# Routing marks and entries built column by column with a scalar per partition, instead of four interleaved columns at a time

## The chip, the cores and the metric

One core of one Trainium2 chip runs the whole program. The metric is device microseconds from launch to end; lower is better. The kernel before takes 689.84 us (median of 3 runs, 689.8 to 689.98).

## What is computed

Attention over 4 batches of 8 heads, 768 positions and 64 features per head, in which each query sees 8 global keys and the last 96 keys, with a linear bias by distance. The result, 3072 tokens of 512 features, goes through a mixture of 8 experts of which each token uses the best two:

```python
logits = x @ w_gate
noisy = logits + log1p(exp(x @ w_noise)) * noise
top2 = np.argpartition(-noisy, 2, axis=1)[:, :2]
top2_w = softmax(noisy at top2)
for e in range(E):
    for k in range(2):
        mask = top2[:, k] == e
        out[mask] += top2_w[mask, k] * (relu(x[mask] @ w1[e]) @ w2[e])
```

## The kernel before, in words

**Attention.** The 24 tiles of 128 tokens are worked through in order, 4 pairs of heads to a tile, two pairs to a turn of the main loop. In a turn TensorE (PE) transposes the attention weights of two pairs (L750), multiplies older ones with the values (L778) and forms the scores of the pairs four further on (L725). VectorE (DVE) adds the bias to the scores and takes the row extreme (L732, once per half pair, followed by a short read of the accumulator); ScalarE (ACT) takes the exponential (L735). After the fourth pair of a tile DVE divides by the row sums (L788 to L790), and PE transposes the tile and forms the gate's logits (L378, L386). Scores and gate products share three PSUM banks in rotation, two for the scores of a turn and one for the gate, so that the scores of pair m are written into the bank out of which DVE read those of pair m - 2. The values' sums have one buffer of their own, which is free again after L790.

**Routing.** The generator `route` turns logits into lists of tokens per expert, in three segments: tiles 0 to 9, 10 to 15 and 16 to 23. Its last part finds for each token and choice a slot, that is an expert's column and a row in it. Per pair of tiles (four choices of 128 tokens each, one product of the matrix multiplier per choice) it builds a `mark` (128 tokens by 128 rows: 1 where the row is the token's) and an `entry` (128 tokens by 64 columns: the token's number where the column is its). Then PE adds up all products mark x entry of the segment (L512), and DVE adds the sum to the table `tab` (L515), from which the lists of tokens are read that the gathers on POOL go by (L521, L527, L288).

A mark is one comparison of 128 x 128 x 4 elements (L502), an entry one comparison of 128 x 64 x 4 (L504) and one multiplication with the tokens' numbers (L506). The fourth dimension, the choice, is innermost, so that a column of one product has a step of 4 elements. `row` and `col` hold the numbers 0 to 127 and 0 to 63, each four times.

**Order of the work.** All engines take their instructions in the program's order. `route` is advanced by its `yield`s: `tick` takes one step between the instructions of the main loop. While the marks are built there is a step after each half pair of scores (four in a turn) and a few more behind them. Within a pair of tiles one step lies behind the mark, one behind the comparison of the entry and one behind its multiplication. So in segments 0 and 1 a step of the marks mostly stands between two L732 on DVE. Segment 2 is taken after the attention, beside the first expert's first layer: `middle` and `after[4]` build the marks of two pairs of tiles at once, and the products L512 are put ahead of the last product of the eighth block of that layer (L1003). Its other DVE work there is L1009 (low half of the hidden layer) and L233 (low half of the second layer's weights). L1058 is the second layer.

Twelve pairs of tiles there are in all: 5, 3 and 4 in the segments, with 20, 12 and 16 products L512. L212 is a later small DVE instruction with a scalar per partition, L177 a 128 x 128 one, L315 and L620 are DVE instructions with constants alone.

Of the kernel before, what the change touches and what calls it, by code (L numbers as in the profile page):

```python
# [10 lines left out]
F32 = mybir.dt.float32  # L11
FR = mybir.dt.float32r
F16 = mybir.dt.float16
# [4 lines left out]
OP = mybir.AluOpType  # L18
AX = mybir.AxisListType

P = 128
NP = 96
TA, TB = 4, 3
TT = TA + TB
# [12 lines left out]
def tile_local_global_attention_then_moe(  # L37
# [13 lines left out]
    nc = tc.nc  # L51
# [6 lines left out]
    E, _, F = w1.shape  # L58
# [3 lines left out]
    NT = B * NB  # L62
# [8 lines left out]
    SW = max(SWS)  # L71

    ctx.enter_context(tc.manual_schedule())
    consts = ctx.enter_context(tc.tile_pool(name="consts", bufs=1))
    small = ctx.enter_context(tc.tile_pool(name="small", bufs=1))
# [4 lines left out]
    gp = wctx.enter_context(tc.tile_pool(name="gp", bufs=1))  # L80
# [28 lines left out]
    turnf = consts.tile([P, E], F32, name="turnf")  # L109
    turni = consts.tile([P, E], I32, name="turni")  # L110
    ids0 = consts.tile([P, 1, TA], I32, name="ids0")
    val16 = consts.tile([P, NT, 2], F16, name="val16")
    row = consts.tile([P, P, 4], F16, name="row")
    col = consts.tile([P, E * (TT + 1), 4], F16, name="col")
    over = consts.tile([P, NT, E], F32, name="over")
    wmx = consts.tile([P, E, 2, 5], F32, name="wmx")
    wex = consts.tile([P, E, 2], F32, name="wex")
# [279 lines left out]
    def route(r):  # L397

        a, z = SEG[r]
        w, sw = z - a, SWS[r % 2]  # L400
        l = lgs[:, a:z]
        u, t, p, ny, po = (small.tile([P, sw, E], F32, name=f"{x}{r % 2}")[:, :w] for x in ("u", "t", "p", "ny", "po"))
        n = l[:, :, E:]
# [30 lines left out]
        for i in range(w + 1):  # L434
# [4 lines left out]
            if i % 2 or r <= CLOSE:  # L439
# [10 lines left out]
                                op=OP.is_equal)  # L450
# [32 lines left out]
        nc.vector.tensor_reduce(sl.rearrange("p t j -> p j t"), oh, op=OP.add, axis=AX.X)  # L483
        yield
        sli = small.tile([P, 2, sw, 2], I32, name=f"sli{r % 2}")[:, :, :w]
        slf = small.tile([P, 2, sw, 2], F16, name=f"slf{r % 2}")[:, :, :w]
        nc.vector.tensor_copy(sli[:, 0], sl)
        nc.vector.tensor_scalar(sli[:, 1], sli[:, 0], 7, None, op0=OP.arith_shift_right)
        yield
# [3 lines left out]
        marks = []  # L493
        K = E * (TT + 1)
        ps = lg[:, HELD * G + (SW + 1) * E:HELD * G + (SW + 1) * E + K]

        for i in range(0, w, 2):
            x = gp.tile([P, P, 4], F16, name="mark", bufs=SW // 2)
            y = gp.tile([P, K, 4], F16, name="entry", bufs=SW // 2)
            here, there = (slf[:, j, i:i + 2].rearrange("p t j -> p (t j)")[:, None] for j in range(2))  # L500
            v = val16[:, a + i:a + i + 2].rearrange("p t j -> p (t j)")[:, None]
            nc.vector.tensor_tensor(x, row, here.to_broadcast([P, P, 4]), op=OP.is_equal)  # L502
            yield "large"
            nc.vector.tensor_tensor(y, col, there.to_broadcast([P, K, 4]), op=OP.is_equal)  # L504
            yield "large"
            nc.vector.tensor_mul(y, y, v.to_broadcast([P, K, 4]))  # L506
            marks += [(x[:, :, k], y[:, :, k]) for k in range(4)]
            yield "marked" if i + 2 in (4, w) else "large"
        for _ in range(4 if r + 1 < len(SEG) else 0):
            yield  # L510
# [5 lines left out]
        if r == CLOSE:  # L516

            nc.vector.tensor_scalar(carry[:, 0:1], carry[:, 0:1], float(CA), None, op0=OP.max)
            x, y = find(None, slice(0, 1), slice(0, TA))
# [9 lines left out]
    def find(to, e, t):  # L529

        v, k = tab[:, e, t], void[:, e, t]
        x, y = (small.tile([P, E, TT + 1], F32, name=f"find{j}")[:, :k.shape[1], :k.shape[2]] for j in range(2))
        nc.vector.tensor_scalar(x, v, 0.0, None, op0=OP.is_equal)
        nc.vector.tensor_scalar(y, v, 0.0, float(DUMP + HALF - 1), op0=OP.is_lt, op1=OP.add)
        nc.vector.tensor_mul(x, x, k)
        nc.vector.tensor_add(y, y, v)
        if to is not None:
            nc.vector.tensor_add(to, x, y)
        return x, y


    with ExitStack() as actx:
# [44 lines left out]
        if windowed:  # L587
# [34 lines left out]
            t = small.tile([P, 1], F32, name="t")  # L622
# [35 lines left out]
        def route_consts():  # L658
            nc.sync.dma_start(noise_s, noise.rearrange("p (t e) -> p t e", e=E))
            nc.vector.memset(upper, 1.0)  # L660
            nc.gpsimd.affine_select(out=upper, in_=upper, pattern=[[1, P]], compare_op=OP.is_gt, fill=0.0,
                                    base=0, channel_multiplier=-1)
            nc.vector.memset(ones, 1.0)
            nc.vector.memset(carry, 0.0)
            nc.gpsimd.memset(zero, 0.0)
            nc.gpsimd.iota(iota_e, pattern=[[0, 1], [1, E]], base=0, channel_multiplier=0,
                           allow_small_or_imprecise_dtypes=True)
            nc.gpsimd.iota(slot0, pattern=[[0, SW], [(TT + 1) * P, E]], base=0, channel_multiplier=0,
                           allow_small_or_imprecise_dtypes=True)
            for h in range(2):  # L670
                nc.gpsimd.iota(val16[:, h * NT // 2:(h + 1) * NT // 2], pattern=[[P, NT // 2], [0, 2]],
                               base=h * (HALF + 1) - HALF, channel_multiplier=1, allow_small_or_imprecise_dtypes=True)
            for t, n, base in (0, TA, 0), (TA, TT + 1 - TA, TA * P - CA):
                nc.gpsimd.iota(void[:, :, t:t + n], pattern=[[0, E], [P, n]], base=base - (DUMP + HALF - 1),
                               channel_multiplier=1, allow_small_or_imprecise_dtypes=True)
            for x in tab, l1, wv, *first:
                nc.vector.memset(x, 0.0)
            for e in range(E):
                nc.gpsimd.memset(room[:, e:e + 1], float(CAPS[e]))

        def mark_consts():
            nc.gpsimd.iota(row, pattern=[[1, P], [0, 4]], base=0, channel_multiplier=0,
                           allow_small_or_imprecise_dtypes=True)
            nc.gpsimd.iota(col, pattern=[[1, E * (TT + 1)], [0, 4]], base=0, channel_multiplier=0,
                           allow_small_or_imprecise_dtypes=True)

        def empty_rows():
# [112 lines left out]
        def whole(g):  # L800
# [60 lines left out]
            for r, (a, z) in enumerate(SEG):  # L861
                if g == z - 1:
                    for _ in route(r):
                        pass

        pending = iter(())
        if not windowed:
            gate_consts()
            route_consts()
            mark_consts()  # L870
            empty_rows()
            for j in range(NZ):
# [15 lines left out]
        else:  # L888
# [3 lines left out]
            for k in range(2, HP):  # L892
                at(k - 2, biases, bias, dist, (2 * k, 2 * k + 1))
            at(4, gate_consts)
            at(10, route_consts)
            at(14, mark_consts)
            at(56, empty_rows)
            for g in range(NT):
                b, i = divmod(g, NB)
                n = g * HP  # L900
                if g + 3 < NT:
                    at(n + 2, load_v, g + 3)
                m = n + HP - 1 + LAG + 1
                if g + 1 < NT:
                    at(m, gate_t, g)
                    at(m + 2, gate_l, g)
                    if g not in held:
                        seen[m + 6] = g
                    elif g + 1 == SEG[CLOSE][1]:
                        then[m + 4] = g  # L910
                    elif m + 4 < NPAIR + LAG:
                        at(m + 4, gate_s, g)
                if i % NBH == 0 and g + NBH < NT:
                    for k in range(NBH):
                        at(n + 4 * k, load_qk, *divmod(g // NBH + 1, 2), k)
                for r, (a, z) in enumerate(SEG):
                    if g == z - 1:
                        routes[m + (4 if g in held else 6)] = [route(r), r, None]
# [427 lines left out]
```

## Time and profile before

| | |
|---|---|
| median of 3 runs | 689.84 us |
| the profiled execution's own time | 687.46 us |
| its span, first to last instruction | 685.7 us |
| granted clock of TensorE, mean | 0.998 |
| attention, routing of segments 0 and 1 | about 0 to 157 us of the span |
| marks of segment 0, 1, 2 on DVE | 108.5 to 116.2, 132.4 to 136.6, 174.2 to 178.9 us |

A matmul's time in the trace includes its way through the array; what one costs in a row of them is the distance of their starts. The same holds on DVE: an instruction starts some 0.08 us before the recorded end of the one ahead of it.

### The profile page before, as it was taken

The page shows a single profiled execution, that of the slowest core. Times are in us where ns is not written, and L with a number is a line of the kernel's source. Part 1 is how long each engine was busy: PE and PEld are TensorE (multiplying, and loading weights), DVE is VectorE, ACT ScalarE, POOL GpSimd, SP SyncE. Part 2 cuts the span into 40 slices and gives each one's busy share as a digit, 9 for nine tenths or more (in the row PEclk, how much of TensorE's full clock was granted, in tenths as well). Part 3 has the DMA queues.
Part 4 walks back from the last instruction along what each step waited for, and adds up shares of the span by engine and source line. Part 5 has one row for each costly group of instructions (what it writes and reads, how often), then busy time and mean ns, then how long its engine had stood idle before and what let it go on. Part 6 is the DMA issues. An engine that isn't in the chain of part 4 may idle for free. (4 is left out here: it accounts for less than half of the span.)

```text
span 685.7 us, 16098 instructions
## 1 busy us (share of the span) xinstructions
PE 674.7 (98%) x6099; PEld 418.9 (61%) x6099; DVE 428.9 (63%) x1455; ACT 366.7 (53%) x830; POOL 195.3 (28%) x208
## 2 busy tenths in 40 slices
PE   7999999999999999999999999999999999999996
PEld 5888878785457665556465746474656466544742
DVE  6686888878958467737572856386547636672600
ACT  6788787885366354625552555256434625442510
POOL 2219510021255712340324032403231331221022
PEclk9999999999999999999999999999999999999999
DMA  8999787949478935954675469438735764471033
GB/s 239 323 309 316 234 253 232 285 151 380 133 137 147 269 124 120 180 139 132 118 171 137 143 99 207 101 124 124 189 93 153 136 168 122 83 107 35 1 40 59
DMA packets 105703, 111.68 MB, mean 163 GB/s; under 512 B 51508, under 2 KB 64468, under 8 KB 105616
## 3 DMA queue, kind: packets, MB, share of 16 engines
q1 hardware_dynamic: 93600, 83.89, 43.1%
q0 software_dynamic: 11472, 26.41, 20.8%
q8 instruction: 50, 0.82, 0.5%
q14 instruction: 37, 0.30, 0.1%
q10 hardware_dynamic: 544, 0.26, 0.1%
HBM read 71.48 MB, written 27.71 MB: 145 GB/s over the span
## 5 line engine op out<-in xcount | busy, mean ns | idle before, releaser
L1003 PEld LDWEIGHTS <-w1h 128*128 128x128 f16 x1024 | 99.7, 98 | 67.2 <-issue 0.8
L1058 PE MATMUL av<-w2h,hh 128*128 128x512 f16 x336 | 127.4, 379 | 0.0
L1058 PE MATMUL av<-w2h,hl 128*128 128x512 f16 x336 | 127.3, 379 | 0.0
L1058 PE MATMUL av<-w2l,hh 128*128 128x512 f16 x336 | 127.3, 379 | 0.0
L1003 PE MATMUL at<-xx,w1h 128*128 128x512 f16 (+5 forms) x512 | 122.9, 330 | 0.6 <-DVE xx L356 0.4
L1003 PE MATMUL sc<-xx,w1h 128*128 128x512 f16 (+5 forms) x512 | 122.8, 330 | 0.0
L1058 PEld LDWEIGHTS <-hh 128*128 128x128 f16 x672 | 65.4, 98 | 76.7
L288 POOL DMA_INDIRECT xg<-xd,ids x54 | 55.2, 1023 | 177.3 <-DVE l L314 92.5
L735 ACT ACTIVATE a<-ns,mx 128x168 f32<-128x168 f32 (+1 forms) x192 | 70.0, 421 | 28.6 <-DVE mx L732 27.4
L1003 PE MATMUL sc<-xx,w1l 128*128 128x512 f16 (+5 forms) x256 | 84.5, 330 | 0.0
L1003 PE MATMUL at<-xx,w1l 128*128 128x512 f16 (+5 forms) x256 | 84.5, 330 | 0.0
L1009 DVE SCALAR_TENSOR_TENSOR hl<-sc,hh 128x512 f16<-128x512 f32 (+5 forms) x64 | 36.2, 565 | 71.7 <-ACT hh L1007 71.7
L171 DVE TENSOR_REDUCE wmx<-raw 128x1 f32<-128x1024 f32 x64 | 75.9, 1206 | 0.0
L1009 DVE SCALAR_TENSOR_TENSOR hl<-at,hh 128x512 f16<-128x512 f32 (+5 forms) x64 | 36.1, 564 | 60.0 <-ACT hh L1007 60.0
L1003 PEld LDWEIGHTS <-w1l 128*128 128x128 f16 x512 | 50.2, 98 | 34.9 <-issue 0.2
L1039 POOL DMA_INDIRECT out_dram<-y,ids x27 | 42.3, 1566 | 102.5 <-ACT y L1038 100.5
L1007 ACT ACTIVATE hh<-at 128x512 f16<-128x512 f32 (+5 forms) x64 | 31.7, 495 | 65.4 <-PE at L1003 65.3
L321 ACT ACTIVATE xp<-xg,up 128x512 f16<-128x512 f32 x48 | 34.2, 720 | 55.5 <-DVE up L315 48.3
L732 DVE CUSTOM_DVE_ANT_0 ns<-sc,bias 128x168 f32<-128x168 f32 (+1 forms) x192 | 53.7, 319 | 16.2 <-PE sc L725 13.0
L1007 ACT ACTIVATE hh<-sc 128x512 f16<-128x512 f32 (+5 forms) x64 | 31.6, 493 | 59.1 <-PE sc L1003 59.1
L1039 POOL DMA_INDIRECT out_dram<-xr,ids x26 | 40.4, 1554 | 74.0 <-ACT xr L1038 73.1
L233 DVE SCALAR_TENSOR_TENSOR w1l<-raw,wsc,w1h 128x512 f16<-128x512 f32 x52 | 36.3, 747 | 36.2 <-ACT w1h L224 35.9
(201 smaller groups left out, 1174.7 us busy)
## 6 DMA issues: line engine op xcount, KB each, us to landing
raw<-in_w SPq DMA_DIRECT2D x28, 1024.0 KB
out_dram<-zero SPq DMA_DIRECT2D x14, 512.0 KB
vs<-in_v SPq DMA_DIRECT2D x24, 260.0 KB
xd<-xr SPq DMA_DIRECT2D x24, 256.0 KB
qs<-in_q SPq DMA_DIRECT2D x23, 256.0 KB
ks<-in_k SPq DMA_DIRECT2D x19, 272.0 KB
raw<-in_w SPq DMA_DIRECT2D x16, 256.0 KB
vp<-in_v SPq DMA_DIRECT2D x20, 195.0 KB
```

What stands on the lines that cost most here:

```text
L171: nc.vector.tensor_reduce(m[:, i:i + 1], t, op=OP.max, axis=AX.X, apply_absolute_value=True)
L233: eng.scalar_tensor_tensor(lo, t, s, hi, op0=OP.mult, op1=OP.subtract)
L288: nc.gpsimd.indirect_dma_start(out=xg[e, t], out_offset=None, in_=xd[:n], in_offset=bass.IndirectOffsetOnAxis(ap=rows(e, t), axis=0), boun ...
L321: nc.scalar.activation(y[:m, :Dm], xg[e, t][:, :Dm], AF.Copy, scale=u)
L732: nc.vector.tensor_tensor_reduce(out=ns[:, s, :w], in0=ps[:, s], in1=bias[:, hp, s] if i else bias0[:, hp, s], scale=-scale, scalar=3e38, ...
L735: nc.scalar.activation(A[m][:, s * w:(s + 1) * w], ns[:, s, :w], AF.Exp, bias=mx[:, s:s + 1], scale=-1.0)
L1003: nc.tensor.matmul(ps, w[e % 2][:, k, fs], xx[c][:, x + k, :z], start=n == 0, stop=n == 3 * KC - 1)
L1007: nc.scalar.activation(hh[c][:, f, :z], ps, AF.Relu)
L1009: nc.vector.scalar_tensor_tensor(hl[c][:, f, :z], ps, 0.0, hh[c][:, f, :z], op0=OP.max, op1=OP.subtract)
L1039: ins = nc.gpsimd.indirect_dma_start(out=out, out_offset=bass.IndirectOffsetOnAxis(ap=rows(e, t), axis=0), in_=y, in_offset=None, bounds_c ...
L1058: nc.tensor.matmul(ps, x[c][:, f, cols], w[e % 2][:, f], start=n == 0, stop=n == 3 * FC - 1)
```

## The change

The four columns of a pair of tiles are made one at a time. A mark's column is a comparison of `row` (128 elements) with a scalar per partition, an entry's column a comparison of `col` (64 elements) with a scalar per partition and, in the same instruction, a multiplication with a second one. Three DVE instructions per pair of tiles become eight. Each product's columns lie side by side in memory. The scalars become 32-bit floats, `row` and `col` a quarter as long. The steps lie behind the third mark, behind the first entry and behind the last entry.

```diff
-    val16 = consts.tile([P, NT, 2], F16, name="val16")
-    row = consts.tile([P, P, 4], F16, name="row")
-    col = consts.tile([P, E * (TT + 1), 4], F16, name="col")
+    val = consts.tile([P, NT, 2], F32, name="val")
+    row = consts.tile([P, P], F16, name="row")
+    col = consts.tile([P, E * (TT + 1)], F16, name="col")
...
-        slf = small.tile([P, 2, sw, 2], F16, name=f"slf{r % 2}")[:, :, :w]
+        slf = small.tile([P, 2, sw, 2], F32, name=f"slf{r % 2}")[:, :, :w]
...
-            x = gp.tile([P, P, 4], F16, name="mark", bufs=SW // 2)
-            y = gp.tile([P, K, 4], F16, name="entry", bufs=SW // 2)
-            here, there = (slf[:, j, i:i + 2].rearrange("p t j -> p (t j)")[:, None] for j in range(2))
-            v = val16[:, a + i:a + i + 2].rearrange("p t j -> p (t j)")[:, None]
-            nc.vector.tensor_tensor(x, row, here.to_broadcast([P, P, 4]), op=OP.is_equal)
-            yield "large"
-            nc.vector.tensor_tensor(y, col, there.to_broadcast([P, K, 4]), op=OP.is_equal)
-            yield "large"
-            nc.vector.tensor_mul(y, y, v.to_broadcast([P, K, 4]))
-            marks += [(x[:, :, k], y[:, :, k]) for k in range(4)]
+            x = gp.tile([P, 4, P], F16, name="mark", bufs=SW // 2)
+            y = gp.tile([P, 4, K], F16, name="entry", bufs=SW // 2)
+            for n in range(8):
+                k = n % 4
+                t, j = i + k // 2, k % 2
+                here, there = (slf[:, m, t, j:j + 1] for m in range(2))
+                if n < 4:
+                    nc.vector.tensor_scalar(x[:, k], row, here, None, op0=OP.is_equal)
+                else:
+                    nc.vector.tensor_scalar(y[:, k], col, there, val[:, a + t, j:j + 1], op0=OP.is_equal, op1=OP.mult)
+                if n in (2, 4):
+                    yield "large"
+            marks += [(x[:, k], y[:, k]) for k in range(4)]
             yield "marked" if i + 2 in (4, w) else "large"
...
-            nc.gpsimd.iota(row, pattern=[[1, P], [0, 4]], base=0, channel_multiplier=0,
+            nc.gpsimd.iota(row, pattern=[[1, P]], base=0, channel_multiplier=0,
-            nc.gpsimd.iota(col, pattern=[[1, E * (TT + 1)], [0, 4]], base=0, channel_multiplier=0,
+            nc.gpsimd.iota(col, pattern=[[1, E * (TT + 1)]], base=0, channel_multiplier=0,
```

## Rows read from the trace of the kernel before

**Rows 1.** The page, part 1: busy time, share of the span, instructions of each engine.

```profile
PE 674.7 (98%) x6099; PEld 418.9 (61%) x6099; DVE 428.9 (63%) x1455; ACT 366.7 (53%) x830; POOL 195.3 (28%) x208
```

**Rows 2.** By stretch: length, busy PE, PEld, DVE, ACT, POOL; marks of segments 0 and 2.

```profile
108.27:126.33 18.06, 18.06 (x338) 14.68 (x338) 16.90 (x109) 14.96 (x42) 0.40 (x2) 1.00 0.87 266
168.40:184.00 15.60, 15.60 (x93) 7.79 (x92) 15.12 (x44) 5.42 (x9) 2.30 (x3) 1.00 0.51 177
```

**Rows 3.** The products L512: engine, op, count, ns min/median/max, first and last start.

```profile
L512 PE MATMUL lg<-entry,mark x48: 223/242/247, 117.4 to 179.9; 128*128 128x64 f16 x48
```

**Rows 4.** Timeline of DVE, segment 0: start us, us, engine, line, op, idle before.

```profile
109.12 0.29 DVE L504 TENSOR_TENSOR entry<-col,slf 128x256 f16<-128x256 f16 x1
109.32 0.33 DVE L732 CUSTOM_DVE_ANT_0 ns<-sc,bias 128x168 f32<-128x168 f32 x1
...
110.03 0.42 DVE L502 TENSOR_TENSOR mark<-row,slf 128x512 f16<-128x512 f16 x1
110.36 0.29 DVE L504 TENSOR_TENSOR entry<-col,slf 128x256 f16<-128x256 f16 x1
110.69 0.29 DVE L506 TENSOR_TENSOR entry<-entry,val 128x256 f16<-128x256 f16 x1
110.91 0.17 DVE L788 TENSOR_SCALAR den<-avb 128x8 f32<-128x8 f32 x1
...
113.32 0.28 DVE L732 CUSTOM_DVE_ANT_0 ns<-sc,bias 128x128 f32<-128x128 f32 x1
...
114.37 0.29 DVE L732 CUSTOM_DVE_ANT_0 ns<-sc,bias 128x128 f32<-128x128 f32 x1 [0.22 <-PE sc L725]
```

**Rows 5.** Timeline of PE: the scores of four turns, merged.

```profile
113.50 0.91 PE L725 MATMUL sc<-ks,qs 64*64 64x128 f32 x15
...
120.29 0.80 PE L725 MATMUL sc<-ks,qs 64*64 64x168 f32 x16
...
126.08 1.04 PE L725 MATMUL sc<-ks,qs 64*64 64x168 f32 x15
...
132.74 1.29 PE L725 MATMUL sc<-ks,qs 64*64 64x168 f32 x15
```

**Rows 6.** Timeline of DVE, then of PE: the marks of segment 1.

```profile
133.92 0.33 DVE L732 CUSTOM_DVE_ANT_0 ns<-sc,bias 128x168 f32<-128x168 f32 x1 [0.30 <-PE sc L725]
...
136.33 0.29 DVE L506 TENSOR_TENSOR entry<-entry,val 128x256 f16<-128x256 f16 x1
...
141.20 0.33 DVE L732 CUSTOM_DVE_ANT_0 ns<-sc,bias 128x168 f32<-128x168 f32 x1 [1.54 <-PE sc L725]
...
137.18 0.91 PE L512 MATMUL lg<-entry,mark 128*128 128x64 f16 x12
```

**Rows 7.** Timeline of DVE, then of PE: the end of segment 2's marks.

```profile
178.66 0.29 DVE L506 TENSOR_TENSOR entry<-entry,val 128x256 f16<-128x256 f16 x1
...
183.20 0.74 DVE L233 SCALAR_TENSOR_TENSOR w2l<-raw,wsc,w2h 128x512 f16<-128x512 f32 x1
...
178.98 1.15 PE L512 MATMUL lg<-entry,mark 128*128 128x64 f16 x16
...
184.94 0.38 PE L1058 MATMUL av<-w2l,hh 128*128 128x512 f16 x1
```

**Rows 8.** DVE instructions with constants (two), and with a scalar per partition.

```profile
L315 DVE TENSOR_SCALAR up<-l x54: 142/153/156, 148.6 to 607.7; 128x1 int32<-128x1 int32 x48, 44x1 int32<-44x1 int32 x3, 20x1 int32<-20x1 int32 x1, 8x1 int32<-8x1 int32 x1
...
L620 DVE TENSOR_SCALAR bias<-dist 64x336 f32<-64x336 f32 x8 | 2.6, 327 | 0.1
...
641.14 0.23 DVE L212 SCALAR_TENSOR_TENSOR yr<-wv,fac,l 128x6 f32<-128x6 f32 x1
641.28 0.42 DVE L1009 SCALAR_TENSOR_TENSOR hl<-at,hh 128x256 f16<-128x256 f32 x1
...
L177 DVE TENSOR_SCALAR dm<-ident,m x16: 286/286/534, 46.3 to 629.6; 128x128 bf16<-128x128 f32 x16
```

**Rows 9.** Timeline of PE: small products whose stationary columns lie side by side.

```profile
101.61 0.39 PE L469 MATMUL lg<-first,ones 128*128 128x72 bf16 x9
```

More of the change, by code (lines that the diff above doesn't have):

```diff
@@ L670, in route_consts @@
             for h in range(2):
-                nc.gpsimd.iota(val16[:, h * NT // 2:(h + 1) * NT // 2], pattern=[[P, NT // 2], [0, 2]],
+                nc.gpsimd.iota(val[:, h * NT // 2:(h + 1) * NT // 2], pattern=[[P, NT // 2], [0, 2]],
                                base=h * (HALF + 1) - HALF, channel_multiplier=1, allow_small_or_imprecise_dtypes=True)
```

## The prediction

> **What bounds the kernel now.** I began with the page's first part: TensorE (PE) is busy for 98% of the span [rows 1], so time is won only where PE gets less work and lost only where it is made to wait. Then the busy time by stretch: around the marks VectorE (DVE) is busy for 16.90 of 18.06 us and for 15.12 of 15.60 us [rows 2]. So the change touches both: the products L512 on the engine that bounds, and the twelve groups of mark and entry on an engine that is nearly full just there. Third, the timelines, for who waits for whom. In the attention the 16 score products of a turn take 0.80 us when nothing holds them [rows 5]. Beside the marks fifteen of them took 0.91 us (though narrower, 128 columns and not 168), 1.04 and 1.29 us: PE stood in them for some 0.3, 0.3 and 0.5 us. The scores go into the bank that DVE has read for the pair two before: the L732 that began at 113.32 and lasted 0.28 us [rows 4] was the last such reading, and the first of the three drawn-out rows runs on both sides of its end. So PE is already at DVE's heels in both attention segments.
>
> **What PE saves.** A product L512 has 64 moving columns. Sixteen take 1.15 us, the last one's own 0.24 included [rows 7, 3]: 0.91 / 15 = 61 ns from start to start. Nine bf16 products of at most 80 columns, whose stationary columns lie side by side, take 0.39 us with a tail of about 0.2 us [rows 9]: some 25 to 30 ns. After the change the stationary columns lie side by side here too; I take 30 ns, as these rows have the same 128 x 128 weights. That is 31 ns x 48 = 1.5 us of PE's work, 0.6, 0.4 and 0.5 us by segment; the bounds are nothing (if the step was not the cause) and this. It counts only where PE does not wait for DVE afterwards.
>
> **What DVE pays.** Before, start to start: mark 0.33 us; comparison of the entry 0.33 us where its multiplication follows at once, 0.20 us where another instruction does; multiplication 0.22 us, about 0.21 elsewhere [rows 4]. A pair of tiles costs 0.74 to 0.88 us, I take 0.75 between scores and 0.87 in a row.
>
> After, eight instructions of a kind the trace lacks: one 16-bit input, scalars per partition. Their price is put together from four rows [rows 8]. A DVE instruction on one element with constants lasts 0.153 us, and 336 f32 elements with a constant 0.327 us: 0.52 ns an element, two a cycle. L212 has 6 elements and a scalar per partition and lasts 0.23 us, 0.07 more than its elements explain. L177 has 128 f32 elements and such a scalar: 0.153 + 128 x 0.52 ns = 0.220, measured 0.286, again 0.066 more. So a scalar per partition costs 0.066 us, and not behind the instruction ahead of it: L212 started at 641.14 and the next at 641.28, that is 0.14 us, where an overlap of some 0.083 is taken off the length. For 16-bit elements I take half the f32 price, 0.26 ns. With two inputs the halving shows: L1009 has 256 f32 elements in 0.42 us, (0.42 - 0.153) / 256 = 1.04 ns [rows 8], and L502 has 256 16-bit elements more than L506 and lasts 0.13 us longer, 0.51 ns [rows 4]. The bounds are 0.26 and 1.04 ns. So a mark's column 0.153 + 0.066 + 0.033 - 0.083 = 0.17 us, an entry's 0.153 + 0.066 + 0.017 - 0.083 = 0.155 us. The entry's second scalar has no row: between 0 and another 0.066. I take 0, both being read for the same start, and keep 0.066 for the range.
>
> By step: three marks 0.51 for 0.34 (+0.17); mark and entry 0.325 for 0.20 or 0.33 (+0.125 or 0); three entries 0.465 for 0.21 (+0.26). A pair of tiles costs 1.3 us: **+0.56 us between scores, +0.43 us in a row**.
>
> The Trainium skill, in VectorE: DVE Perf Modes (sections on the perf-mode tier table and on the TRN2 errata), has a 16-bit tensor_scalar handle four elements a cycle at a fixed 58 cycles a piece, whatever its scalar is. As an estimate from that page a pair of tiles would cost 4 x (58 + 32) + 4 x (58 + 16) cycles at 0.96 GHz, 0.68 us, and the sum would be near that of the second rival below; the extra 0.066 us of L212 and L177 speaks against it.
>
> **Segment 0 (5 pairs).** Four are between scores, one in a row: 4 x 0.56 + 0.43 = 2.67 us. DVE idles 0.22 us at 114.37 [rows 4], which takes in what comes between the bank's release and that start, and about 0.1 us elsewhere before PE stands again at 126.08 [rows 5]. All the rest goes into the bank waits: **+2.3 us**. PE's 0.6 us fall into the same waits and are lost.
>
> **Segment 1 (3).** The first three marks stand ahead of the bank for which PE waits at 132.74 [rows 5]: +0.17. The remainder of that pair of tiles, 0.26, fits into DVE's idle 0.30 before 133.92 [rows 6]. The second and third pair make DVE late by about 1.0 us more. Between none and all of it could reach PE; I take none of it by way of the scores, since DVE waits 1.54 us for those before 141.20 [rows 6], so that PE is not held by it there. And the last entry, 136.33 + 0.29 + 1.15 = 137.8 us, comes when PE is through with eight of the twelve products that it begins at 137.18 [rows 6]; these are shorter by 0.4 in all, so that the wait eats what they save. **+0.15 us.** The first gathers on POOL start a microsecond later; the layer that reads their rows begins only with the end of the attention, near 157 us.
>
> **Segment 2 (4).** DVE has next to no idle time here [rows 2], so 4 x 0.43 = 1.7 us arrive in full. The last entry ends at 178.95 + 1.7 = 180.65 us [rows 7]. PE now ends its products at 178.98 + 0.91 + 0.06 = 179.95; it would end them 0.07 us (a semaphore) and four products later than that entry: 180.85. **+0.9 us.** Behind it L233, done at 183.94 + 1.7 = 185.6, is wanted by L1058 at 184.94 + 0.9 = 185.8 [rows 7]: just in time. The tiles gathered from the finished table are wanted after the first four tiles of L1058, so a gather 1.7 us late is covered.
>
> **The rest is nothing.** The shorter `row` and `col` save POOL three quarters of two iotas near 27 us, long before they are read; `val` and `slf` have as many elements as before; no DMA, no queue and no wait is moved, the steps stay three per pair of tiles.
>
> Sum 2.3 + 0.15 + 0.9 = 3.35, say **+3.4 us**. The profiled execution, 687.46 us, would be 690.9; the median stands 2.4 us above it, and 689.84 + 3.4 = **693.2 us**.
>
> **The rivals.**
> (1) *The second scalar is read after the first.* An entry's column is 0.22 us, a pair of tiles 1.55 us: +0.82 and +0.69. Segment 0: 4 x 0.82 + 0.69 - 0.3 = 3.7. Segment 1: the slack of the next scores is used up, and the last entry holds the products, about 0.85. Segment 2: 2.76 late, of which 0.85 are in hand, 1.9. Together +6.5: 696.3 us. For it: the first scalar is not hidden either. Against it: no row has two.
> (2) *The scalars are free in this short form, not slower.* Then 0.10 and 0.087 us a column, 0.76 us a pair of tiles: +0.0 and -0.11. DVE is no later, PE's 0.6 us of segment 0 still end in the bank wait at 126.08, and those of segments 1 and 2 come through: -0.1 - 0.4 - 0.5 = -1.0, 688.8 us. It decides below about 0.125 us a column, where DVE's lateness in segment 0 no longer outweighs PE's gain. L212 and L177 are against it; that both are other forms, in f32, is for it. The Trainium skill's page named above (VectorE: DVE Perf Modes, errata) would have it so. Its far end, all of PE's 1.5 us, is 688.3.
> (3) *The fast element rate doesn't come.* At one 16-bit element a cycle: 0.27 and 0.20 us a column, 1.9 us a pair of tiles, +1.14 and +1.0. Segments 5.3, 1.4 and 3.2: +9.9, 699.7 us. Against it: L620 and L177 run at two a cycle even in f32.
> (4) *The products don't get shorter*, because the step was not what held them: in my forecast only some 0.2 us hang on it, since DVE decides; 693.4 us.
>
> **How the numbers follow.** Forecast 0.42 (with the fourth, which ends in the same place), first rival 0.25, second 0.22, third 0.06, something unseen 0.05. A measurement of this kernel can tell about 0.2%, 1.4 us, from no change. The second rival lies mostly within that (0.17) and by a part beyond (0.05); the unseen I split: faster 0.07, same 0.20, slower 0.73. The range takes in forecast, first and second rival, 688.8 to 696.4; the forecast's own is 692 to 694.5.
>
> **What would show it.** In the profile after, eight DVE instructions per pair of tiles, those of the mark near 0.25 us and of the entry near 0.24 us long; at 0.31 the first rival holds, at 0.19 and 0.17 the second. L512 near 30 ns apart. The score products near 113.5 and 126 drawn out by about 2 us together, and PE idle for about a microsecond ahead of the last L512 of segment 2. I am wrong if PE's wait there is missing, or if the marks of segment 0 end no later than now.

## The result and the profile after

The changed kernel takes **696.26 us** (median of 6 runs, 694.79 to 696.93), the kernel before 689.91 us on the same chip (6 runs, 689.71 to 690.47). The ratio is 1.0086, with an interval of 1.0076 to 1.0096: **6.35 us slower**, somewhere between 5.2 and 6.6. The direction was right, and the time lies in the range, just inside its upper end (696.4). The forecast, 693.2 us, was about half of the way; the first rival's 696.3 us was the time that came.

The page's first part, against [rows 1]:

```profile
PE 679.2 (98%) x6099; PEld 420.2 (60%) x6099; DVE 437.1 (63%) x1515; ACT 366.8 (53%) x830; POOL 193.9 (28%) x208
```

DVE has 60 instructions more (five more for each of 12 pairs of tiles) and is busy for 8.2 us more. The span grew from 685.7 to 694.8 us. In the new code L505 is the mark's column, L507 the entry's, L515 the products, L728 the scores, L735 the bias and row extreme, L791 to L793 the divisions, L1006 and L1061 the two layers.

The three new kinds of instruction, from the views of these lines (count, shortest/median/longest in ns, first and last start, form):

```profile
L505 DVE TENSOR_SCALAR mark<-row,slf x48: 244/248/259, 110.9 to 188.0; 128x128 f16<-128x128 f16 x48
L507 DVE TENSOR_SCALAR entry<-col,slf,val x48: 290/296/304, 111.8 to 188.7; 128x64 f16<-128x64 f16 x48
L515 PEld LDWEIGHTS <-mark x48: 94/98/99, 122.1 to 188.9; 128*128 128x128 f16 x48
L515 PE MATMUL lg<-entry,mark x48: 188/193/202, 122.1 to 189.1; 128*128 128x64 f16 x48
```

The mark's column lasts 248 ns, as forecast (0.25 us). The entry's column lasts **296 ns, though it has half as many elements**; the forecast was 0.24 us, and 0.31 was to speak for the first rival. The products fell from 242 ns [rows 3] to 193 ns.

DVE in segment 0, one pair of tiles in a row, against [rows 4] (start, us, instruction; equal neighbours are merged):

```profile
113.16 0.74 DVE L505 TENSOR_SCALAR mark<-row,slf 128x128 f16<-128x128 f16 x4
113.81 0.91 DVE L507 TENSOR_SCALAR entry<-col,slf,val 128x64 f16<-128x64 f16 x4
114.64 0.15 DVE L791 TENSOR_SCALAR den<-avb 128x8 f32<-128x8 f32 x1
```

Four marks take 113.81 - 113.16 = 0.65 us, four entries 0.83 us: 0.163 and 0.206 us from start to start. The pair costs 1.48 us, 0.88 before [rows 4].

Who waits for that is seen in PE's timeline of the scores, against [rows 5]:

```profile
116.94 0.38 PE L728 MATMUL sc<-ks,qs 64*64 64x128 f32 x3
...
118.22 0.65 PE L728 MATMUL sc<-ks,qs 64*64 64x128 f32 x12 [0.90 <-DVE mx L735]
...
125.72 0.79 PE L728 MATMUL sc<-ks,qs 64*64 64x168 f32 x12 [0.21 <-DVE p L422]
```

PE's waits in that trace from 110 to 152 us (engine, line, what it waited for: us in total, times, longest):

```profile
PE sc L728 <- DVE mx L735: 1.1, 2, 0.9
PE avb L781 <- DVE xr L793: 0.4, 2, 0.2
PE sc L386 <- ACT xt L380: 0.4, 2, 0.2
PE avb L781 <- issue: 0.2, 1, 0.2
PE sc L728 <- DVE p L422: 0.2, 1, 0.2
```

The same list in the second profile of before (109 to 149 us) has one entry:

```profile
PE sc L725 <- issue: 0.3, 1, 0.3
```

An `issue` is a stop for which the profile names nothing. This one lies in the last scores of the attention, and up to 147 us the list of before is empty:

```profile
148.95 0.52 PE L725 MATMUL sc<-ks,qs 64*64 64x168 f32 x4 [0.26 <-issue]
```

PE now stands between the fourth and the fifth score product until DVE has read the bank (L735): 0.90 us at once, where [rows 5] showed products drawn out by 0.3. The engines behind wait in turn: the values' sums for the division, the gate for ACT's copy.

In segment 2, against [rows 7], the timeline of PE's products and then of DVE's last pair of tiles:

```profile
186.60 1.20 PE L515 MATMUL lg<-entry,mark 128*128 128x64 f16 x12
188.47 0.81 PE L515 MATMUL lg<-entry,mark 128*128 128x64 f16 x4 [0.67 <-DVE entry L507]
189.12 0.38 PE L1006 MATMUL sc<-xx,w1l 128*128 128x512 f16 x1
...
187.47 0.73 DVE L505 TENSOR_SCALAR mark<-row,slf 128x128 f16<-128x128 f16 x4
188.12 0.91 DVE L507 TENSOR_SCALAR entry<-col,slf,val 128x64 f16<-128x64 f16 x4
```

PE is through with twelve products and waits 0.67 us for the last entries, as foreseen; before, sixteen ran without a stop.

For the sizes by stage I compared starts of the same instructions in two traces: the scores of the turn ahead of the marks, the last division of segment 0's stretch, the first layer's first product, the second layer's first, the end. As the kernel before I took its second profile (the fifth experiment); the first was 2.2 us shorter, half of it ahead of the marks and half late in the attention. The table gives the microseconds gained (-) or lost (+) in each stretch.

| kernel | up to the marks | segment 0 | segment 1 | segment 2 | behind | span |
|---|---|---|---|---|---|---|
| before, first profile | -1.10 | 0.00 | -1.14 | -0.01 | 0.0 | -2.24 |
| **after** | +1.29 | **+3.07** | **+1.01** | **+1.52** | -0.07 | +6.82 |
| marks alone | +1.57 | +1.07 | +0.62 | +0.62 | -0.07 | +3.81 |
| entries alone | +0.82 | +2.01 | +0.33 | +0.34 | -0.31 | +3.19 |
| two by two | +0.54 | -0.18 | -0.12 | -0.51 | -0.29 | -0.56 |
| third scalar | +1.14 | +4.26 | +1.81 | +2.50 | +1.74 | +11.45 |
| POOL multiplies | +0.25 | -0.51 | -0.10 | -0.51 | -0.31 | -1.18 |
| segment 2 alone | +0.31 | -0.01 | 0.00 | +1.53 | -0.30 | +1.53 |

The three segments of the changed kernel give 3.07 + 1.01 + 1.52 = **5.6 us**, which the medians' interval of 5.2 to 6.6 holds; the rest, ahead of the marks, scatters from profile to profile. The first row tells how far two executions of one kernel differ: by nothing in the segments 0 and 2, but by 1.14 us in segment 1, most of it in the last scores of the attention. So the column of segment 1 decides nothing below about a microsecond.

The forecast had 2.3 + 0.15 + 0.9, the first rival 3.7 + 0.85 + 1.9. The rival is too high in the segments 0 and 2; that its total met the median to a tenth is in part luck.

### The profile page after: what moved, and what is told of

It is laid out like the page before. It is cut to its first block, busy times and chain, and to the rows that moved or that the text cites. A ratio compares the mean times of both kernels' runs of the same rounds, so it can differ in the third digit from the quotient of the medians.

```text
span 694.8 us, 16158 instructions
## 1 busy us (share of the span) xinstructions
PE 679.2 (98%) x6099; PEld 420.2 (60%) x6099; DVE 437.1 (63%) x1515; ACT 366.8 (53%) x830; POOL 193.9 (28%) x208
## 5 line engine op out<-in xcount | busy, mean ns | idle before, releaser
L1006 PEld LDWEIGHTS <-w1h 128*128 128x128 f16 x1024 | 99.5, 98 | 67.4 <-issue 0.8
L1061 PE MATMUL av<-w2h,hh 128*128 128x512 f16 x336 | 127.5, 379 | 0.0
L1061 PE MATMUL av<-w2h,hl 128*128 128x512 f16 x336 | 127.5, 379 | 0.0
L1061 PE MATMUL av<-w2l,hh 128*128 128x512 f16 x336 | 127.5, 379 | 0.0
L1006 PE MATMUL at<-xx,w1h 128*128 128x512 f16 (+5 forms) x512 | 123.0, 330 | 0.5 <-ACT xx L355 0.4
L1006 PE MATMUL sc<-xx,w1h 128*128 128x512 f16 (+5 forms) x512 | 122.9, 330 | 0.0
L1061 PEld LDWEIGHTS <-hh 128*128 128x128 f16 x672 | 65.3, 98 | 76.8
L1006 PE MATMUL sc<-xx,w1l 128*128 128x512 f16 (+5 forms) x256 | 84.6, 330 | 0.0
L1006 PE MATMUL at<-xx,w1l 128*128 128x512 f16 (+5 forms) x256 | 84.6, 330 | 0.0
L1006 PEld LDWEIGHTS <-w1l 128*128 128x128 f16 x512 | 50.1, 98 | 35.1 <-issue 0.2
L735 DVE CUSTOM_DVE_ANT_0 ns<-sc,bias 128x168 f32<-128x168 f32 (+1 forms) x192 | 53.8, 319 | 18.1 <-PE sc L728 14.5
L233 DVE SCALAR_TENSOR_TENSOR w1l<-raw,wsc,w1h 128x512 f16<-128x512 f32 x52 | 36.3, 748 | 36.3 <-ACT w1h L224 36.0
```

Source lines behind the costliest of these rows:

```text
L233: eng.scalar_tensor_tensor(lo, t, s, hi, op0=OP.mult, op1=OP.subtract)
L735: nc.vector.tensor_tensor_reduce(out=ns[:, s, :w], in0=ps[:, s], in1=bias[:, hp, s] if i else bias0[:, hp, s], scale=-scale, scalar=3e38, ...
L1006: nc.tensor.matmul(ps, w[e % 2][:, k, fs], xx[c][:, x + k, :z], start=n == 0, stop=n == 3 * KC - 1)
L1061: nc.tensor.matmul(ps, x[c][:, f, cols], w[e % 2][:, f], start=n == 0, stop=n == 3 * FC - 1)
```

## The experiments

**One half of the change at a time.** The marks alone in the new form:

```diff
-            x = gp.tile([P, P, 4], F16, name="mark", bufs=SW // 2)
+            x = gp.tile([P, 4, P], F16, name="mark", bufs=SW // 2)
...
-            nc.vector.tensor_tensor(x, row, here.to_broadcast([P, P, 4]), op=OP.is_equal)
-            yield "large"
+            for k in range(4):
+                t, j = i + k // 2, k % 2
+                nc.vector.tensor_scalar(x[:, k], row, slh[:, t, j:j + 1], None, op0=OP.is_equal)
+                if k == 2:
+                    yield "large"
```

> The marks alone as in the change (four columns, one scalar each, side by side); the entries as before; one more cast of 20 or fewer elements per segment. Theory (a scalar per partition costs DVE some 0.065 us, and what DVE is late by turns up in PE's waits): mark columns 0.163 us apart, 0.65 us per pair of tiles where the mark before took 0.34, so +0.31 us; segment 0 +1.3 us, segment 1 +0.2, segment 2 1.25 late of which about 1.0 is in hand, +0.3: 1.8 us slower than before, 691.7 us. If the step of the stationary columns was what held L512, its products are 30 ns apart here too; if the moving ones held it, they stay at 60. Rival (only the second scalar of the entries is dear, the first is hidden among the rest of the work): no slower than before, 689 to 690 us.

Measured 693.4 us (693.24 to 694.25), ratio 1.0052 [1.0038, 1.0065]: +3.1 us. The view of the products' line:

```profile
L517 PE MATMUL lg<-entry,mark x48: 217/239/241, 121.0 to 186.0; 128*128 128x64 f16 x48
```

PE's timeline, segment 0's twenty:

```profile
120.98 1.36 PE L517 MATMUL lg<-entry,mark 128*128 128x64 f16 x20
```

Twenty products in 1.36 us, the last one's 0.24 taken off, are 59 ns from start to start. The stationary columns (the marks) lie side by side here, and **the products are as slow as before**. The 3.1 us are more than the theory's 1.8: the segments give 2.3 of it (1.07, 0.62 and 0.62, where 1.3, 0.2 and 0.3 were expected), the rest lies ahead of the marks. The rival, no loss from the first scalar, is out.

The entries alone in the new form, the marks interleaved as before:

```diff
-            y = gp.tile([P, K, 4], F16, name="entry", bufs=SW // 2)
+            y = gp.tile([P, 4, K], F16, name="entry", bufs=SW // 2)
...
-            nc.vector.tensor_tensor(y, col, there.to_broadcast([P, K, 4]), op=OP.is_equal)
-            yield "large"
-            nc.vector.tensor_mul(y, y, v.to_broadcast([P, K, 4]))
+            for k in range(4):
+                t, j = i + k // 2, k % 2
+                nc.vector.tensor_scalar(y[:, k], col, slt[:, t, j:j + 1], val[:, a + t, j:j + 1], op0=OP.is_equal, op1=OP.mult)
+                if k == 0:
+                    yield "large"
```

> The entries alone as in the change (four columns, two scalars each); the marks as before, interleaved; one more cast of 20 or fewer elements per segment. Theory: entry columns 0.206 us apart, 0.82 us where the two instructions of before took 0.41 between scores and 0.53 in a row: +0.41 and +0.29 us; segment 0 +1.6, segment 1 +0.3, segment 2 1.2 late of which 0.75 is in hand, +0.4: 2.3 us slower than before, 692.2 us; L512 stays at 60 ns if the stationary columns' step holds it. Rival (the second scalar carries all of the loss): 6 us slower, 696 us.

Measured 692.88 us (691.12 to 693.58), ratio 1.0038 [1.0025, 1.005]: +2.6 us. The line's view:

```profile
L515 PE MATMUL lg<-entry,mark x48: 189/198/218, 120.6 to 185.7; 128*128 128x64 f16 x48
```

Segment 0's products in PE's timeline:

```profile
120.60 0.85 PE L515 MATMUL lg<-entry,mark 128*128 128x64 f16 x20
```

(0.85 - 0.20) / 19 = 34 ns. So it is the **moving** operand, the entries, whose step of 4 elements holds the products; the marks' step alone costs 4 ns. The two halves lose 5.7 us together, near the whole, so that neither carries the loss alone, as its rival (6 us from the entries) had it; each carries one more conversion per segment, since it needs the scalars in both types.

**PE's saving without DVE's price.** The same three instructions as before, with the choices interleaved by two and not by four, so that a product's columns have a step of 2:

```diff
-    row = consts.tile([P, P, 4], F16, name="row")
-    col = consts.tile([P, E * (TT + 1), 4], F16, name="col")
+    row = consts.tile([P, 2, P, 2], F16, name="row")
+    col = consts.tile([P, 2, E * (TT + 1), 2], F16, name="col")
...
-            x = gp.tile([P, P, 4], F16, name="mark", bufs=SW // 2)
-            y = gp.tile([P, K, 4], F16, name="entry", bufs=SW // 2)
+            x = gp.tile([P, 2, P, 2], F16, name="mark", bufs=SW // 2)
+            y = gp.tile([P, 2, K, 2], F16, name="entry", bufs=SW // 2)
...
-            marks += [(x[:, :, k], y[:, :, k]) for k in range(4)]
+            marks += [(x[:, k // 2, :, k % 2], y[:, k // 2, :, k % 2]) for k in range(4)]
```

> The operations of before (three per pair of tiles, two tensors each), but the two choices of one token tile interleaved and the two tiles side by side: a step of 2 elements in place of 4 in the products. Theory: DVE pays what it paid (0.34, 0.20, 0.21 us), since it still reads neighbouring 16-bit elements, and L512 comes closer together, between 30 and 60 ns; as DVE decides in segment 0, some 0.3 to 0.9 us come through in segments 1 and 2: 689.0 to 689.9 us. Rival (DVE's price hangs on the long run of four): marks of 0.6 us, about 4 us slower.

Measured 689.12 us (11 runs, 688.58 to 689.86) against 690.3 (17 runs), ratio 0.9985 [0.9976, 0.9994]: **1.1 us faster than before**, by the ratios 1% faster than the change, and inside what the theory expected. The line's view:

```profile
L512 PE MATMUL lg<-entry,mark x48: 190/193/203, 119.0 to 181.9; 128*128 128x64 f16 x48
```

PE's timeline: segment 0's products, and the scores that follow two steps behind them:

```profile
119.02 0.77 PE L512 MATMUL lg<-entry,mark 128*128 128x64 f16 x20
...
121.28 0.92 PE L725 MATMUL sc<-ks,qs 64*64 64x168 f32 x9
```

30 ns a product: a step of 2 costs PE nothing. DVE's three instructions last as long as before. By the starts, the trace is 0.60 us ahead when segment 0's products are through, and has given 0.42 of it back by the end of the stretch: nine scores take 0.92 us, where sixteen take 0.80 when nothing holds them [rows 5], because DVE has not read the bank any sooner. Only segment 2 keeps all of its saving, 0.51 us (16 x 31 ns). The forecast's sentence that PE's 0.6 us "fall into the same waits and are lost" is thus shown for 0.42 of the 0.60, with nothing else changed.

**One more scalar.** The marks of the changed kernel get a second scalar, a multiplication by a column of ones:

```diff
-                    nc.vector.tensor_scalar(x[:, k], row, here, None, op0=OP.is_equal)
+                    nc.vector.tensor_scalar(x[:, k], row, here, one, op0=OP.is_equal, op1=OP.mult)
```

> The changed kernel with a second scalar per partition, a one, multiplied into each mark's column: no instruction more, only a scalar more. Theory: mark columns 0.225 us apart in place of 0.163, 0.25 us more per pair of tiles, all of it after DVE's slack is used up: segment 0 +1.2, segment 1 +0.5, segment 2 +1.0: 2.7 us above the changed kernel, 699.0 us. Rival (what is dear is the number of instructions, and the entries' length comes from the multiplication of the elements): mark columns stay at 0.163 to 0.18 us, 696.3 us.

Measured 699.69 us (698.53 to 701.35), ratio to before 1.0142 [1.0125, 1.0159], 3.4 us above the change where 2.7 were expected. The mark's line:

```profile
L506 DVE TENSOR_SCALAR mark<-row,slf,one x48: 302/306/313, 110.8 to 190.7; 128x128 f16<-128x128 f16 x48
```

306 ns for 248: the second scalar costs 0.06 us. From start to start it is 0.224 for 0.163 us, 0.244 us a pair of tiles; segment 0 should lose 5 x 0.244 = 1.22 us more and loses 4.26 - 3.07 = 1.19, segment 2 should lose 0.98 and loses 0.98, segment 1 0.73 and 0.80. **What DVE is late by reaches PE in full** from here on, clearly so in the segments 0 and 2. The rival (the number of instructions) is out. The 1.74 us behind segment 2 are another matter, told in the last section.

**Before, once more**, because the start of the first profile of before lay ahead of the change's:

> The kernel before once more, for a second profile of it: the profiled execution shown ended 2.4 us ahead of the median, and its first tiles came 1 to 2.7 us earlier than in all five other profiles. Theory: that lead lies in when the first loads land and has nothing to do with the change; this profile has the sixth tile's scores near 42 to 43 us as the others have, and the stretches of the marks as the first profile. Rival: the later start belongs to the changed kernels; this profile has them at 40.7 us again.

Its span is 688.0 us, its own time 689.78. The scores of the sixth tile began at 41.77 us, between the two numbers expected. In the first profile they began at 40.67, in the changed kernel's at 43.07, in those of six other kernels of this study at 42.0 to 43.4: the start scatters by over 2 us among kernels that do the same there. Where in that the kernel before belongs isn't settled by two profiles; for this reason the segments are compared and not the spans.

**The prices by themselves.** 48 small instructions of the same kind on DVE and 60 products behind the kernel's end, with results that nobody reads:

```diff
+        for n in (P, 64):
+            for s1, s2 in ((1.0, 1.0), (sa[:, 1:2], 1.0), (sa[:, 1:2], sa[:, 2:3])):
+                for k in range(8):
+                    nc.vector.tensor_scalar(po[:, k, :n], pr[:, :n], s1, s2, op0=OP.is_equal, op1=OP.mult)
...
+        for w, x in ((stf[:, :P], mvf[:, :64]), (stf[:, :P], mv[:, :, 0]), (st2, mvf[:, :64]), (st[:, :, 0], mvf[:, :64]),
+                     (st[:, :, 0], mv[:, :, 0])):
+            for n in range(12):
+                nc.tensor.matmul(ps, w, x, start=n == 0, stop=n == 11)
```

> The kernel before with 48 small DVE instructions and 60 small products behind its last work, each kind in a row, results not used. Theory: a 16-bit tensor_scalar with constants 0.10 us from start to start at 128 elements and 0.085 at 64; with one scalar per partition 0.163 and 0.147; with two 0.225 and 0.206, each scalar some 0.06. Products of 64 moving columns: 28 to 30 ns with both side by side; near 60 ns wherever the moving columns have a step of 4 elements, whatever the stationary ones have; near 34 ns where the stationary ones alone have it. Rival: the scalars' price is that of two operations in one instruction, so that constants with two operations cost as much as two scalars; and the stationary step holds the products.

DVE's timeline: two constants, one scalar and two scalars with 128 elements, then the same with 64 (of the eight of a kind, the six to eight that the row's stretch holds):

```profile
682.81 0.80 DVE L1313 TENSOR_SCALAR hl<-ident 128x128 f16<-128x128 f16 x7
683.62 1.22 DVE L1313 TENSOR_SCALAR hl<-ident,iota_e 128x128 f16<-128x128 f16 x7
684.92 1.65 DVE L1313 TENSOR_SCALAR hl<-ident,iota_e 128x128 f16<-128x128 f16 x7
686.71 0.60 DVE L1313 TENSOR_SCALAR hl<-ident 128x64 f16<-128x64 f16 x6
687.39 1.11 DVE L1313 TENSOR_SCALAR hl<-ident,iota_e 128x64 f16<-128x64 f16 x7
688.55 1.74 DVE L1313 TENSOR_SCALAR hl<-ident,iota_e 128x64 f16<-128x64 f16 x8
```

PE's timeline: both operands side by side, the moving one alone at a step of 4, the stationary one alone at a step of 4, both at a step of 4:

```profile
683.13 0.51 PE L1319 MATMUL sc<-w2l,w2h 128*128 128x64 f16 x12 [1.03 <-DVE hl L1313]
683.48 0.76 PE L1319 MATMUL sc<-w2l,w2h 128*128 128x64 f16 x10
686.43 0.40 PE L1319 MATMUL sc<-w2l,w2h 128*128 128x64 f16 x7
686.85 0.91 PE L1319 MATMUL sc<-w2l,w2h 128*128 128x64 f16 x12
```

With the last one's own length taken off (186, 248 and 309 ns; 173, 233 and 296), the distances are **0.102, 0.162 and 0.223 us** with 128 elements and **0.086, 0.146 and 0.206 us** with 64. Each scalar per partition costs 0.060 to 0.061 us, the second as much as the first. A second operation with a constant costs nothing: one scalar with it takes 0.162 us here, one scalar without it 0.163 us in the changed kernel. So the rival, the price of two operations, is out. All scalars here and in the change are 32-bit; shorter ones were not run. Elements are nearly free: 64 more cost 0.016 us.

The products: 29 ns with both operands side by side, 29 with the stationary one at a step of 2, 33 to 34 with it at a step of 4, and 60 between most starts with the moving one alone at a step of 4 (behind its tenth product PE stops for 1.69 us). The last row tells nothing of the step, since it ran at half the clock:

```profile
686.85:687.30 0.45, 0.45 (x12) 0.45 (x10) 0.45 (x7) 0.00 (x0) 0.00 (x0) 0.50 0.15 36
```

That is the busy time of its first part by engine, with a granted clock of 0.50; the products of the rows above it started at 1.00. For both operands at a step of 4 there are the kernel before's 61 ns, at a granted clock of 1.00 [rows 2, 7].

**The entries' multiplication on POOL**, on top of two by two, to see how much is left to win if DVE gets less to do:

```diff
-            nc.vector.tensor_mul(y, y, v.to_broadcast([P, K, 4]))
+            nc.gpsimd.tensor_mul(y, y, v.to_broadcast([P, 2, K, 2]))
```

> Two by two as in e3, and the entries' multiplication with the tokens' numbers is done by POOL instead of DVE. Theory (DVE's length in the marks is what PE waits for): 0.21 us less per pair of tiles on DVE; segment 0 gains up to 1 us of the bank waits, segment 1 up to 0.3, so some 1 us below e3, 688 us. Rival (DVE and POOL hold each other up, or POOL is too slow for the last entry of segment 2): DVE's marks grow longer or PE waits for the last product; 690 us or more.

Measured 689.18 us (11 runs, 688.37 to 690.22), ratio 0.999 [0.998, 0.9999]: no better than two by two as far as the intervals can tell, so that the 1 us expected below it didn't come. The view of the multiplication's line:

```profile
L506 POOL TENSOR_TENSOR entry<-entry,val x12: 610/614/730, 110.8 to 180.5; 128x256 f16<-128x256 f16 x12
```

A mark in DVE's timeline, while POOL multiplies:

```profile
114.67 0.64 DVE L502 TENSOR_TENSOR mark<-row,slf 128x512 f16<-128x512 f16 x1
```

In segment 0 PE now keeps 0.51 us of its saving (0.18 without POOL), as a less loaded DVE should allow; the other segments are the same. Four of DVE's twelve marks and two of its entries' comparisons get longer, each while a multiplication runs on POOL: 0.46 to 0.70 us, here 0.64 for 0.42 [rows 4]. That is 1.4 us in all on DVE, of about 2.5 (12 x 0.21) that it no longer spends on the multiplications.

**The change in segment 2 alone**, the other two as before:

```diff
+            if r == 2:
...
+                        nc.vector.tensor_scalar(x[:, k], row1, here, None, op0=OP.is_equal)
...
+                continue
```

> The change in segment 2 alone, segments 0 and 1 as before. Theory (each stretch pays for its own DVE time): the last entry of segment 2 is 2.4 us late, of which 0.8 is in hand: 1.5 us slower than before, 691.7 us, with PE's wait ahead of the last four products. Rival (segment 2 only hands on what was lost before it): as before, 690.2 us.

Measured 691.76 us (690.73 to 692.02), ratio 1.0026 [1.0014, 1.0037]: +1.9 us, as the theory had it. PE's products:

```profile
181.53 1.21 PE L531 MATMUL lg<-entry,mark 128*128 128x64 f16 x12
183.40 0.81 PE L531 MATMUL lg<-entry,mark 128*128 128x64 f16 x4 [0.67 <-DVE entry L513]
```

The same wait of 0.67 us as in the whole change, and 1.53 us in the table for 1.52: the segments add up, and what segment 2 loses doesn't hang on the lateness of the others.

## Why the prediction was right in direction and too small

**DVE sets the time, PE's saving doesn't: right.** PE waits for L735 in the attention and for the last entries in segment 2, where the prediction put both. With the scalars' price left out (two by two) the kernel gets faster, with one more scalar slower by the amount that DVE gets later.

**The price of a mark: right.** 0.17 us forecast, 0.163 measured. A scalar per partition was read from two quite other instructions [rows 8] as 0.066 us and is 0.060.

**The price of an entry: the term that was mis-sized.** "The entry's second scalar has no row: between 0 and another 0.066. I take 0, both being read for the same start". It is the other end, 0.06 us: 0.206 us for 0.155. That is 4 x 0.05 = 0.2 us a pair of tiles, which is, but for the marks' 0.03, the difference between the forecast's +0.56 and the +0.73 measured (1.48 for 0.75), or +0.43 and +0.61 in a row. The reason given for 0, that both are read for the same start, had nothing in the trace for it; the one fact at hand, that the first scalar isn't hidden, was on the other side, and the prediction itself set it down for the rival.

The forecast's own sums with these prices: segment 0, 4 x 0.73 + 0.61 - 0.3 = 3.2 (3.07 measured); segment 2, 4 x 0.61 = 2.4 late with 0.85 in hand, 1.6 (1.52 measured). So the slacks of these two segments were read rightly and the price was not. Of the 2.2 us that the segments lost beyond the forecast's 3.35, 1.4 lie there, the rest in segment 1.

The Trainium skill, in VectorE: DVE Perf Modes (the tier table and the TRN2 errata), was weighed with 0.68 us a pair of tiles. Its four 16-bit elements a cycle, 0.26 ns an element at its 0.96 GHz, agree with the runs: 0.016 us for 64 elements are 0.25 ns each. Its fixed 58 cycles, 0.060 us at 0.96 GHz, are near the 0.070 us that these rows leave (0.102 - 128 x 0.25 ns). But each scalar adds 0.06 us, on which those sections have nothing, and twelve of them in a pair of tiles are 0.73 us, the difference to the 1.48 us measured but for 0.07. The measurement decides.

**Segment 1: +0.15 forecast, +1.01 measured.** The wait for the bank is there as foreseen: +0.15 us at the scores where 0.17 was expected. By the first product the delay is 0.41 us. The products then take as long as before, from first to last 0.67 us, because the last entry ends only at 142.74 + 0.92 = 143.66 us and the last product starts at 143.04 + 0.67; their saving is eaten, also as foreseen:

```profile
143.04 0.86 PE L515 MATMUL lg<-entry,mark 128*128 128x64 f16 x12
...
142.74 0.92 DVE L507 TENSOR_SCALAR entry<-col,slf,val 128x64 f16<-128x64 f16 x4
```

The last 0.65 us arise in one stretch of the values' products, in which PE stops at 149.17 us for 0.44 and the profile names nothing that it waits for:

```profile
149.17 0.22 PE L781 MATMUL avb<-vs,at 64*64 64x65 f32 x1
149.61 0.21 PE L781 MATMUL avb<-vp,at 40*64 40x65 f32 x1 [0.22 <-issue]
```

The entries alone and the third scalar lose 0.54 and 0.63 us in the same stretch, the marks alone nothing. What it is stays open, and it is less than the 1.14 us by which the two profiles of before differ in this segment; so only the 0.41 us are sure to be the change's. The forecast's argument, DVE's own wait for the scores ahead of 141.20 [rows 6], shrank to 0.52 us but was not used up. The rival's 0.85 was nearer; whether for its reason, a used-up slack, is not shown, and this stretch scatters by more than the two differ.

**What PE saves: right in size, wrong in its cause.** 30 ns were forecast and 30 came, since the change lays both operands side by side. But the step said: the stationary columns, by the likeness to [rows 9]. The marks alone show that these are not what held the products, and the entries alone that the moving ones are. The rows could not tell the two apart, because both have a step of 4 before and a step of 1 in [rows 9]. The fourth rival (no shortening) is out; that it would have changed little was not run by itself.

**L233 and the gathers of segment 2: right.** Behind segment 2 nothing is lost (-0.07 us).

## What to carry to other kernels

Price a short DVE instruction with one 16-bit input as a fixed part plus one part for each scalar per partition, before its elements: here 0.07 + 0.06 for each + 0.25 ns an element, so that eight small ones with twelve scalars cost 1.48 us where three large ones without any cost 0.75 to 0.88. Where interleaving for DVE's sake makes a product slow, look at the moving operand first and try a smaller step: interleaved by two, neither engine paid. And where PE follows at another engine's heels, a saving on PE counts only in the stretch in which nothing waits for that engine afterwards.

## What the hardware showed that was not expected

**A step of the moving operand.** 64 columns of 16 bits at a step of 1 or 2: 29 to 30 ns a product; at a step of 4: 59 to 61 ns. The stationary operand alone at a step of 4: 33 to 34 ns. All of these ran at a granted clock of 1.00.

**TensorE's clock after short waits.** In the kernel with the third scalar PE waits 0.73 and 0.91 us for entries, shortly after one another. Its timeline:

```profile
189.56 0.81 PE L516 MATMUL lg<-entry,mark 128*128 128x64 f16 x4 [0.73 <-DVE entry L508]
191.28 0.81 PE L516 MATMUL lg<-entry,mark 128*128 128x64 f16 x4 [0.91 <-DVE entry L508]
```

The busy time by stretch (length, busy PE, PEld, DVE, ACT, POOL, granted clock, DMA share, GB/s):

```profile
190.00:191.20 1.20, 0.35 (x2) 0.16 (x2) 1.20 (x7) 0.00 (x0) 0.00 (x0) 1.00 0.00 0
191.20:192.10 0.90, 0.77 (x5) 0.46 (x5) 0.90 (x5) 0.00 (x0) 0.00 (x0) 1.00 0.00 0
192.10:193.00 0.90, 0.90 (x4) 0.34 (x3) 0.90 (x2) 0.60 (x1) 0.00 (x0) 0.74 0.00 0
193.00:194.00 1.00, 1.00 (x4) 0.40 (x3) 0.97 (x4) 0.00 (x0) 0.00 (x0) 0.50 0.00 0
...
196.00:197.00 1.00, 1.00 (x6) 0.47 (x5) 0.96 (x4) 0.00 (x0) 0.70 (x2) 1.00 0.00 0
```

After the waits the granted clock falls from 1.00 to 0.50, that is from 2.4 to 1.2 GHz, and is back by 196 us, although PE is busy without a break from 192.1 on. Products of the second layer start 0.427 us apart there and 0.216 us in the changed kernel at the same place; that is the 1.74 us behind segment 2 in the table. This profiled execution took 701.23 us, with a granted clock of 0.996 in the mean of its span. Of the other four runs three had 0.993 (701.35, 699.69 and 699.59 us) and one 0.999 (698.53); no run of any other kernel of this study is below 0.997. So the clock fell in four runs of five, and part of the 3.4 us above the change is likely its doing. The changed kernel, with one wait of 0.67 us, keeps its clock. In the run of the prices it fell as well, within a microsecond after the stop of 1.69 us. That the waits bring it down is likely from this and not shown.
